# Strassen's scheme in the second MLP product of the four-block chunks (sliding-window attention and an MLP on one NeuronCore)

## The chip, the cores and the metric

The kernel runs on one core of a Trainium2 chip. The metric is device time in microseconds (us) of one execution, lower is better. Three runs of the kernel before took 319.13, 319.74 and 320.32 us; their median is 319.74.

The engines are named as in the profile: PE is TensorE (PEld its weight loads), DVE is VectorE, ACT is ScalarE, POOL is GpSimd, SP is SyncE, which here only issues DMAs. Each engine works through its own queue in order. PE writes its products to PSUM, in banks of 512 fp32 values per partition; the other engines take them from there.

## The reference

Attention over 8 batches, 8 heads, 576 positions and a head size of 64, in a window of 128 positions back with a linear bias for each head; its output, 4608 rows of 512, goes through a norm and a two-layer MLP of width 2048 and is added to the result:

```python
scores = np.where(mask, q @ k.T / sqrt(64) + bias, -1e9)     # mask: 0 <= rel < 128
x = softmax(scores) @ v                                      # 8 x 576 x 512
xn = (x - mean(x)) / sqrt(var(x) + 1e-6) * g_ln
out = x + np.maximum(xn @ w_ch1, 0.0) @ w_ch2                # w_ch1 512 x 2048, w_ch2 2048 x 512
```

## The kernel before

The 4608 rows are 36 blocks of 128. For each block `attention(i)` loads q, k and v, transposes q and k, makes the scores (L750, for the early blocks with a bias product at L766), their exponentials (ACT, L798), the masking product (DVE, L805), the weighted values (L822, two halves of four heads), and on DVE the division by the sums (L839, L843), the statistics (L864, L870) and the centred, scaled rows `xs` (L876, L883). `xs` is transposed into `xt`, for the first blocks on PE and later by a DMA from SP's queue (L912). The DMAs for q, k and v of the later blocks are cast in flight and issued from POOL's queue (L499); q and k of later blocks are transposed by DMA from SP's queue (L729).

The MLP (`mlp(c)`, L932) runs over ten chunks of 3, 3, 2 and then seven times 4 blocks. The first product, 16 groups of four matmuls (L944), makes 128 of the 2048 hidden columns each, for all rows of the chunk at once (512 columns of moving data in a four-block chunk). ACT or DVE applies the ReLU on the way from PSUM to `ht` in fp16 (L956, L954). The second product takes one block after the other: 16 matmuls of 512 columns (L972), with a 128x128 piece of `ht` as weights and a row piece of `w_ch2` (`w2sb`) as moving data, summed in one bank of PSUM. DVE scales the sum by the row's 1/std (the norm's division is left until here), adds `xb`, the attention output (L980, written `o` with the block's number), and SP's queue stores the result (L988). The last block's product is cut into 384 and 128 columns.

The order of all this is not written out. `Plan` is a list scheduler that runs when the program is built: every piece is a task with an engine or a choice of engines (`add(name, {"ACT": cost, "DVE": cost}, ...)`), the tasks that it waits for, and a due time `v`; for each engine the ready task with the earliest due time comes next. So an added task can change the order around it. The attention of a block has a due time some 1.6 chunks before that of its MLP, so in the middle of the kernel the attention of later blocks lies between the products of a chunk. `PRI`, `HOLD` and `PICK` are tables of hand-set corrections to due times, earliest starts and choices of engine, by the tasks' names.

PSUM has eight banks. `scs` are two tiles of two banks each for scores; `fb` are four banks for everything else: a task takes a bank with `acq` and the task named in `rel` frees it. A `Ring` is a set of buffers that are used in turn: the next use of a buffer waits for the readers of the last. `ht` has two buffers, `ot` (the output rows) four, `xs` three, `qkt` (transposed q and k) six and more for single blocks.

Of the kernel before, what the change touches and what calls it, by code (L numbers as in the profile page):

```python
# [241 lines left out]
def kernel(  # L242
# [17 lines left out]
    NKB = d_model // P  # L260
    NFB = ffn // P
    HP = H // 2
    NBLK = B * S // P
    PERIOD = 2 * S // P
    CB = 4
    CH = CB * P
    CHUNKS = [3, 3, 2, 4, 4, 4, 4, 4, 4, 4]
    FIRST = [sum(CHUNKS[:c]) for c in range(len(CHUNKS))]
# [38 lines left out]
    def sb(name, shape, dt):  # L307
        return pool.tile(shape, dt, tag=name, name=name)
# [10 lines left out]
    iden32 = sb("iden32", [P, P], FP32)  # L319
    sid = sb("sid", [P, H, P], FP16)  # L320
    dist_t = sb("dist_t", [P, 3, 2 * P], FP16)
# [11 lines left out]
    k32 = ring("k32", 2, [P, H, D if single else 1], FP32)  # L333
    v32 = ring("v32", min(4, V_CAST), [P, H, D], FP32)
    qk16 = ring("qk16", 5, [P, 2, d_model], FP16)
    vx = ring("vx", 7 if V_CAST > 4 else 9, [P, H, VD], FP16, FAR)
    qkt = ring("qkt", 6, [P, 2, HP, P], FP16, FAR)
    qs = ring("qs", 2, [P, H, 2 * D], FP32)
    ks = ring("ks", 2, [P, H, 2 * D], FP32)
    qs16 = ring("qs16", 2, [P, H, D, 2], FP16)  # L340
    ks16 = ring("ks16", 2, [P, H, D, 2], FP16)
    probs = ring("probs", 3, [P, 4, 2, 2 * P], FP16)
# [3 lines left out]
    ht = ring("ht", 2, [P, NFB, CH], FP16)  # L346
    ot = ring("ot", 4, [P, d_model], FP32)
    st = ring("st", 4, [P, nc.vector.BN_STATS_DIM], FP32)
# [5 lines left out]
    mean = ring("mean", 4, [P, 1], FP32)  # L354
    g_row, one_t = ot[3][0:1, :], ot[2][0:1, 0:P]

# [8 lines left out]
    def av(i, stage=0.0):  # L365
        return (i / CB - LEAD) * SPAN + stage
# [187 lines left out]
    def weights(i, casts):  # L554

        for n, at in enumerate(W_AFTER):
# [9 lines left out]
            t_w[n] = plan.transfer(f"w{n}", "POOL", 0.8, (3.2 if n else 4.2) if n < 4 else 2.7, 0.0, emit, [casts[at % 3]] + last, av(i, -60.0))  # L566

    span_done, pv_done, qkt_part, first_turn = {}, {}, {}, []
    qkt_done, vx_done, aggr_done, xs_done, xt_done = {}, {}, {}, {}, {}

    def attention(i):
# [49 lines left out]
        if i < V_CAST:  # L621
            cv = [add(f"cv{i}", pick("cv", "POOL", POOL=0.64, ACT=0.62), e_cv, lv_, av(i, 0.2))]
            v32.reads(i, cv[0]); vx.writes(i, cv[0])
        else:
            cv = lv_
# [9 lines left out]
        if i in span_of:  # L635
            n = span_of[i]
            if SPANS[n] == i:
                evs, casts = [[], []], {}
                for (a, x), (landed, h0, h1) in span_load[n].items():
                    r_, w_ = ((qs, qs16), (ks, ks16))[a]  # L640

                    def e_c(e, b, r_=r_, w_=w_, n=n, h0=h0, h1=h1):
                        dst = w_[n][:, h0:h1, :, :].rearrange("p h d t -> p t h d")
                        src = r_[n][:, h0:h1, :].rearrange("p h (t d) -> p t h d", t=2)
                        if e == "ACT":
                            nc.scalar.activation(out=dst, in_=src, func=AF.Copy)
                        else:
                            (nc.vector if e == "DVE" else nc.gpsimd).tensor_copy(out=dst, in_=src)  # L648
                    f = (h1 - h0) / H
                    cs = add(  # L650
                        f"cT{i}.{a}{x}", pick(f"cs{a}{x}", "POOL", POOL=0.12 + 1.26 * f, ACT=0.22 + 1.18 * f, DVE=0.1 + 0.7 * f),
                        e_c, [landed], av(i, 0.1 * a + 0.2 * x),
                    )
                    r_.reads(n, cs); w_.writes(n, cs)
                    for y in range(2) if f == 1 else (x,):
                        casts[a, y] = cs
                for x in range(2):
# [10 lines left out]
                    first_turn.append(tt)  # L668
                    qs16.reads(n, tt); ks16.reads(n, tt)
                    for blk in range(2):  # L670
                        def e_ev(e, b, x=x, blk=blk, key=key):
# [105 lines left out]
        for halves in ((0,), (1,)) if i < SPLIT else ((0, 1),):  # L777
# [4 lines left out]
            if bias:  # L782
                z_ = [add(f"Z{tag}{i}", ("PE", (0.87 if r else 0.46) * part), e_z(halves), t_sid + d_dist[kind > 0], av(i, 1.5 + 0.6 * halves[0]), acq=acq)]
            st_ = add(f"S{tag}{i}", ("PE", 0.19 + (0.45 if r else 0.23) * part), e_s(halves), z_ + qkt_part[i][halves[0]] + ([] if r == 0 else qkt_part[before][halves[0]]), av(i, 2.0 + 0.6 * halves[0]), acq=acq)
            qkt.reads(i, st_)
# [132 lines left out]
        if j == CHUNKS[c] - 1:  # L918
# [11 lines left out]
            kept[c] = rs  # L930

    def mlp(c):  # L932
        nb = CHUNKS[c]
        n_ = nb * P
        done = [xt_done[FIRST[c] + n] for n in range(nb)]
        v0, per = FIRST[c] / CB * SPAN, nb / CB * SPAN / 32
        relu = []
        for f in range(NFB):
            key = f"A{c}.{f}"
            vm = v0 + f * per  # L940

# [16 lines left out]
            ht.writes(c, r_)  # L958
            relu.append(r_)
        for j in range(nb):  # L960
            i = FIRST[c] + j
            cuts = (0, 3 * P, d_model) if i == NBLK - 1 else (0, d_model)
            for c0, c1 in zip(cuts, cuts[1:]):
                key = f"B{i}" if c1 - c0 == d_model else f"B{i}.c{c0}"
                last = None
                for f0 in range(0, NFB, 4):
                    vm = v0 + 16 * per + (4 * j + f0 / 4 + c0 / 100) * SPAN / 32

                    def e_b(e, b, j=j, f0=f0, key=key, c0=c0, c1=c1):
                        pm = fb[plan.held[key][1]]  # L970
                        for f in range(f0, f0 + 4):
# [3 lines left out]
                            )  # L975
                    last = add(f"{key}.{f0}", ("PE", 0.864 * (c1 - c0) / d_model), e_b, relu[f0 : f0 + 4] + [t_w[4 + f0 // 4][1], last], vm, acq=("fb", key))
                    ht.reads(c, last)
# [21 lines left out]
    for n, (at, tasks) in enumerate(cast_seq):  # L999
        before = [t_w[m][0] for m, w_at in enumerate(W_AFTER) if (w_at // 3 * 3 + 2 if w_at // 3 in span_of else w_at) < at][-1:] + (cast_seq[n - 1][1] if n and at < 3 * LOAD_CAST else [])  # L1000
        for t in tasks:
            t.deps += before
    t_g.deps.append(first_turn[0])
    for c in range(len(CHUNKS)):
        mlp(c)
# [46 lines left out]
```

## Time and profile before

| what | us |
|---|---|
| median of three runs (319.13 to 320.32) | 319.74 |
| span of the profiled execution | 317.5 |
| ScalarE busy in it | 161.0 |
| GpSimd busy in it | 100.6 |
| second product, L972, all forms: busy | 134.6 |
| first product, L944, all forms: busy | 134.5 |
| weighted values, L822, from `vx`: busy | 27.2 |
| scores, L750, largest two groups: busy | 18.0 and 14.7 |
| output step on VectorE, L980, all forms: busy | 27.2 |
| division, L843, and masking, L805 (all forms): busy | 30.3 each |

The profile is of one execution; the span goes from its first to its last instruction, and a run's time lies some 2 us above it. A line such as `L972 PE MATMUL fb<-w2sb,ht 128*128 128x512 f16 x560 | 131.6, 379 | 0.1` names the source line, the engine, the operation, what it writes from what it reads, the shape (128 partitions, 512 columns), the count, busy us and mean ns of one, and the engine's idle time before. Matmuls overlap in PE's pipeline, so the mean of one is longer than the time that one adds. In the chain, each piece has its start, its length, the engine and the line.

### The profile page before, as it was taken

How to read it: one execution, taken by the hardware profiler on the slowest of the kernel's cores; microseconds unless marked ns; L12 is line 12 of the kernel's file. 1: busy time of each engine (PE TensorE's matmuls, PEld its weight loads, DVE VectorE, ACT ScalarE, POOL GpSimd, SP SyncE). 2: the span in 40 equal slices, each digit the busy share in tenths (PEclk: the TensorE clock that was granted, in tenths of full speed). 3: DMA queues.
4: the chain of work that ended last, by engine and by line, in shares of the span. 5: the costliest groups of instructions: out<-in, count | busy, mean ns of one | idle time of the engine just before them, and what ended most of it. 6: DMA issues, size and time to landing. Idle time of an engine off the chain costs nothing.

```text
span 317.5 us, 6575 instructions
## 1 busy us (share of the span) xinstructions
PE 311.3 (98%) x2580; PEld 178.3 (56%) x2580; DVE 189.5 (60%) x523; ACT 161.0 (51%) x258; POOL 100.6 (32%) x133
## 2 busy tenths in 40 slices
PE   8999999999999999999999999999999999999995
PEld 7777656765955544555555555545555455445543
DVE  3496788889866646764676467648654676221012
ACT  3657816872836732674267426742574257305600
POOL 5663469765633355434263234000000000000000
PEclk9999999999999999999999999999999999999999
DMA  8999999999999999999999999834600240011011
GB/s 176 248 219 205 196 140 167 168 148 117 162 178 158 174 138 173 171 166 131 171 189 154 100 135 172 108 52 116 118 17 19 83 85 18 21 66 66 2 66 66
DMA packets 156049, 40.15 MB, mean 126 GB/s; under 512 B 142577, under 2 KB 151025, under 8 KB 156018
## 3 DMA queue, kind: packets, MB, share of 16 engines
q0 software_dynamic: 101680, 16.65, 75.7%
q1 hardware_dynamic: 54336, 23.08, 40.9%
q8 instruction: 20, 0.33, 0.5%
q14 instruction: 11, 0.09, 0.1%
q10 hardware_dynamic: 2, 0.00, 0.0%
HBM read 36.70 MB, written 9.44 MB: 145 GB/s over the span
## 4 chain that ended last, share of the span: by engine, by line
PE 91%; DMA 5%; DVE 1%; SPq 0%; POOL 0%; issue 0%
PE fb L944 40%; PE fb L972 39%; PE sc L750 6%; PE fb L822 5%; DMA vxp<-in_v_dram 3%; DMA qs<-in_q_dram 2%; PE fb L714 1%; PE fb L1011 0%; SPq L483 0%; PE fb L897 0%; PE sc L766 0%; PE fb L666 0%; POOL qs L648 0%; POOL w1sb L562 0%; DVE mmix L469 0%
## 5 line engine op out<-in xcount | busy, mean ns | idle before, releaser
L972 PE MATMUL fb<-w2sb,ht 128*128 128x512 f16 (+2 forms) x592 | 134.6, 373 | 0.1
L944 PE MATMUL fb<-xt,w1sb 128*128 128x512 f16 (+2 forms) x640 | 134.5, 359 | 0.0
L956 ACT ACTIVATE ht<-fb 128x512 f16<-128x512 f32 (+2 forms) x142 | 79.5, 560 | 52.4 <-PE fb L944 50.7
L798 ACT ACTIVATE probs<-sc 128x1024 f16<-128x1024 f32 (+1 forms) x72 | 67.8, 973 | 69.2 <-PE sc L750 69.0
L944 PEld LDWEIGHTS <-w1sb 128*128 128x128 f16 x640 | 68.9, 114 | 47.1
L972 PEld LDWEIGHTS <-ht 128*128 128x128 f16 x592 | 54.0, 98 | 57.4 <-issue 0.3
L980 DVE SCALAR_TENSOR_TENSOR ot<-fb,rstd,xb 128x512 f32<-128x512 f32 (+2 forms) x37 | 27.2, 736 | 42.1 <-PE fb L972 41.8
L499 POOL DMA_DIRECT2D vx<-in_v_dram x36 | 30.4, 849 | 38.0 <-PE fb L822 21.1
L499 POOL DMA_DIRECT2D qk<-in_q_dram x34 | 28.5, 839 | 42.7 <-DMA qkt<-qk 22.6
L805 DVE TENSOR_TENSOR probs<-probs,mreg 128x1024 f16<-128x1024 f16 (+1 forms) x46 | 30.3, 676 | 13.9 <-ACT probs L798 13.7
L839 DVE RECIPROCAL rec<-fb 128x4 f32<-128x4 f32 x72 | 12.7, 179 | 36.7 <-PE fb L822 36.4
L822 PEld LDWEIGHTS <-probs 128*128 128x128 f16 x544 | 24.9, 97 | 13.1 <-issue 0.6
L843 DVE SCALAR_TENSOR_TENSOR xb<-fb,rec 128x256 f16<-128x256 f32 x72 | 30.3, 422 | 1.9
L499 POOL DMA_DIRECT2D qk<-in_k_dram x34 | 28.7, 847 | 7.0 <-DMA qk<-in_k_dram 2.1
L883 DVE SCALAR_TENSOR_TENSOR xs<-xb,mean,g_t 128x512 f16<-128x512 f16 x36 | 26.9, 748 | 0.7
L822 PE MATMUL fb<-vx,probs 128*128 128x65 f16 x496 | 27.2, 193 | 0.1
L864 DVE BATCH_NORM_STATS2 st<-xb 128x6 f32<-128x512 f16 x36 | 24.6, 683 | 0.0
L750 PEld LDWEIGHTS <-qkt 64*128 64x128 f16 x496 | 14.9, 94 | 11.9 <-issue 10.1
L750 PE MATMUL sc<-qkt 64*128 64x128 f16 x264 | 18.0, 216 | 0.0
L750 PE MATMUL sc<-qkt,qkt 64*128 64x128 f16 x208 | 14.7, 219 | 0.0
L954 DVE TENSOR_SCALAR ht<-fb 128x384 f16<-128x384 f32 (+2 forms) x18 | 10.4, 579 | 6.3 <-PE fb L944 6.0
L1011 PE MATMUL fb<-warm_t 128*128 128x128 f16 x122 | 10.6, 251 | 1.1 <-DVE warm_t L400 1.1
(71 smaller groups left out, 128.6 us busy)
## 6 DMA issues: line engine op xcount, KB each, us to landing
out_dram<-ot SPq DMA_DIRECT2D x35, 256.0 KB, 4.0
vx<-in_v_dram POOLq DMA_DIRECT2D x28, 128.0 KB, 9.8
qk<-in_q_dram POOLq DMA_DIRECT2D x26, 128.0 KB, 9.2
qk<-in_k_dram POOLq DMA_DIRECT2D x26, 128.0 KB, 10.1
w1sb<-in_moe_w_ch_dram POOLq DMA_DIRECT2D x4, 512.0 KB, 11.1
w2sb<-in_moe_w_ch_dram POOLq DMA_DIRECT2D x4, 512.0 KB, 14.2
ks<-in_k_dram SPq DMA_DIRECT2D x4, 256.0 KB, 6.5
qs<-in_q_dram SPq DMA_DIRECT2D x4, 256.0 KB, 6.2
```

The costliest lines, as they stand in the source:

```text
L499: nc.gpsimd.dma_start(out=dst(p0, n), in_=src[b, :, s0 : s0 + n, :].rearrange("h p d -> p h d"))
L750: nc.tensor.matmul(scs[half][:, g, c0 : c0 + P], kt[rows, 1, hp, :], qkt[i][rows, 0, hp, :], start=not bias, stop=True, skip_group_check=True,
L798: nc.scalar.activation(out=o, in_=n_, func=AF.Exp, scale=inv_sqrt_d)
L805: en.tensor_tensor(out=pv, in0=pv, in1=mask[:, 2 * half : 2 * half + 2, :, lo:], op=ALU.mult)
L822: nc.tensor.matmul(pp[:, hh * (D + 1) : hh * (D + 1) + D + 1], probs[i][:, bank, slot, side * P : side * P + P], vx[i if side else before] ...
L843: nc.vector.scalar_tensor_tensor(out=xb[i][:, 256 * half : 256 * half + 256].rearrange("p (h d) -> p h d", d=D), in0=pp[:, :, 0:D], scalar ...
L864: nc.vector.bn_stats(out=st[i][:, :], in_=xb[i][:, :])
L883: nc.vector.scalar_tensor_tensor(out=xs[i][:, :], in0=xb[i][:, :], scalar=mean[i][:, 0:1], in1=g_t[:, :], op0=ALU.subtract, op1=ALU.mult,)
L944: nc.tensor.matmul(fb[b][:, 0:n_], w1f[f // CB][:, kb, f % CB, :], xt[c][:, kb, 0:n_], start=(kb == 0), stop=(kb == NKB - 1),)
L956: nc.scalar.activation(out=ht[c][:, f, 0:n_], in_=src, func=AF.Relu)
L972: nc.tensor.matmul(pm[:, 0 : c1 - c0], ht[c][:, f, j * P : j * P + P], w2sb[f // CB][:, f % CB, c0:c1], start=(f == 0), stop=(f == NFB - 1),)
L980: nc.vector.scalar_tensor_tensor(out=ot[i][:, c0:c1], in0=fb[plan.held[key][1]][:, 0 : c1 - c0], scalar=rstd[c][:, j : j + 1], in1=xb[i][: ...
```

## The change

For the seven four-block chunks the second product becomes one step of Strassen's scheme (in Winograd's form). The chunk's `ht` is seen as a matrix of four quarters: rows of its first two blocks and its last two (`lo_`, `hi_`), hidden columns 0 to 1023 and 1024 to 2047; `w_ch2` as four quarters too: the two halves of the hidden rows and of the 512 columns. Seven products of quarters (P1 to P7) take the place of eight. Each is 2 blocks x 8 hidden tiles = 16 matmuls of 256 columns.

- `weight_sums` makes four quarter sums of `w2sb` (`tw`, eight DVE instructions of 128x1024 fp16), once.
- `second` makes four quarter sums of `ht` in each chunk: `s3`, `s2`, `s1` (in place, over the lower left quarter) and `s4`, each in two halves of the hidden tiles, so eight DVE instructions of 128x1024 fp16. A half waits for the ReLUs of its eight hidden tiles, and the ReLUs of the second half end with the last one of the chunk.
- The products share four banks: P1 and then P2 in bank a, P6 and P7 in b, P5 and P3 in c, P4 in d. Between two products of one bank the first's value is taken out: `t1` copies P1 (ACT or DVE), `u2` = P6 + t1, `u3` = (P6 + P7) + t1, `v22` = P5 + u3, `v21` = P4 + u3, `v12` = (P5 + P3) + u2, all fp32 on DVE from PSUM, 512 columns at once (two blocks).
- Finishing steps (scale, add `xb`): `o11` for P1 + P2 from PSUM and `o12` from SBUF, 256 columns for each of two blocks, `o2`, 512 columns from SBUF, for each of the other two.
- The order of the products is 1, 6, 2, 7, 5, 4, 3. In the last chunk it is 1, 6, 7, 5, 4, 3, 2, each product is split by block, c and d are the score banks, and the results of the first two blocks are stored in two halves.
- The first product's hidden tiles are made in the order 0, 8, 1, 9, ... .
- To make room, the buffers `qs`, `ks`, `qs16`, `ks16`, `sid` and `v32` of the early blocks share their memory with the sums; `gate` holds the sums until all early users are done.

The planner gives every choice among the finishing steps to DVE, and all `t1` to ACT. `PRI`, `HOLD` and `PICK` stay as they are.

```diff
-    CHUNKS = [3, 3, 2, 4, 4, 4, 4, 4, 4, 4]
+    FOLDED = {c for c, n in enumerate(CHUNKS) if n == 4}
...
+    def weight_sums():
+        for m in range(2):
+            part = [t[:, CB * m : CB * m + CB, :] for t in tw]
+            landed = [t_w[4 + m][1], t_w[6 + m][1]]
+            steps = (
+                (0, quarter(0, 1, m), quarter(0, 0, m), ALU.subtract, None),
+                (1, quarter(1, 1, m), part[0], ALU.add, 0),
+                (2, quarter(0, 1, m), quarter(1, 1, m), ALU.add, None),
+                (3, quarter(1, 0, m), part[1], ALU.subtract, 1),
+            )
...
+    def second(c, relu, v0):
+        for g in range(2):
+            f_, f2 = slice(CB * g, CB * g + CB), slice(HFB + CB * g, HFB + CB * g + CB)
+            ready = [relu[f] for f in range(CB * g, CB * g + CB)] + [relu[HFB + f] for f in range(CB * g, CB * g + CB)]
+            steps = (
+                ("s3", s3[:, 0, f_, :], h[:, f_, hi_], h[:, f_, lo_], []),
+                ("s2", s3[:, 1, f_, :], h[:, f2, hi_], s3[:, 0, f_, :], ["s3"]),
+                ("s1", h[:, f_, hi_], h[:, f_, hi_], h[:, f2, hi_], ["s3"]),
+                ("s4", s3[:, 2, f_, :], h[:, f2, lo_], s3[:, 1, f_, :], ["s2"]),
+            )
...
+        PRODUCTS = {
+            1: ("a", hq(0, 0), w2q(0, 0), None, None),
+            2: ("a", hq(0, 1), w2q(1, 0), None, None),
+            6: ("b", sq(1), tq(1), "s2", 1),
+            7: ("b", sq(0), tq(2), "s3", 2),
+            5: ("c", hq(1, 0), tq(0), "s1", 0),
+            3: ("c", sq(2), w2q(1, 1), "s4", None),
+            4: ("d", hq(1, 1), tq(3), None, 3),
+        }
+        last_one = c == len(CHUNKS) - 1
+        wide_banks = "cd" if last_one else ""
+        groups = [[p] for p in range(np_)] if last_one else [list(range(np_))]
+        order_ = (1, 6, 7, 5, 4, 3, 2) if last_one else (1, 6, 2, 7, 5, 4, 3)
...
+                                nc.tensor.matmul(
+                                    pm[:, k_ * HALF_D : k_ * HALF_D + HALF_D], left(f, p), right(f),
+                                    start=begins and k_ == 0 and f == 0, stop=f == HFB - 1, skip_group_check=True,
+                                )
...
+                    nc.vector.tensor_tensor(out=dst, in0=a, in1=i1, op=ALU.add)
+                return add(name, ("DVE", 0.14 + 0.55 * share), emit, deps, vv, rel=keys[x] if rel and x not in wide_banks else None)
...
+                    t_["u"] = after["b"] = vec(f"u2{c}.{gn}", "b", tile_of["t"], tile_of["u"], [tail, t_["t"]] + gate, v - 4.0)
...
+                    t_["w"] = vec(f"u3{c}.{gn}", "b", tile_of["t"], tile_of["w"], [tail, t_["t"]] + gate, v - 4.0, rel=True)
...
+                            nc.vector.scalar_tensor_tensor(out=dst, in0=src, scalar=scale, in1=xb[i][:, c0:c1], op0=ALU.mult, op1=ALU.add)
...
     def mlp(c):
...
+        for at, f in enumerate([f for n in range(HFB) for f in (n, n + HFB)] if folded else range(NFB)):
...
+        if folded:
+            second(c, relu, v0 + 16 * per)
+            return
         for j in range(nb):
```

## The prediction

> **What bounds the kernel now.** I read the page's busy shares and slices first, then the chain that ended last, then the windows by stage, then the groups with the shapes kept apart, then pieces of the timeline.
>
> ```profile
> span 317.5 us, 6575 instructions
> PE 311.3 (98%) x2580; PEld 178.3 (56%) x2580; DVE 189.5 (60%) x523; ACT 161.0 (51%) x258; POOL 100.6 (32%) x133
> ...
> PEclk9999999999999999999999999999999999999999
> ```
>
> TensorE (PE) is busy 98% of the span at the full granted clock. A busy PE need not be at its peak, so the chain has to say whether the products themselves fill the time. Its last three pieces are two second products with a first product between them, 64 matmuls each (80 in the last, where one block is cut in two):
>
> ```profile
> 272.50 13.81 PE fb L972 x64
> 286.31 13.81 PE fb L944 x64
> 300.13 13.87 PE fb L972 x80
> ```
>
> 13.81 / 64 = 0.216 us for a matmul of 512 columns, with no gaps. So a matmul removed from the second product (L972) shortens the span by its own time, as long as nothing else becomes late. The windows show who might:
>
> ```profile
> core 0: us, PE busy (x) PEld busy (x) DVE busy (x) ACT busy (x) POOL busy (x), PEclk, DMA share, GB/s
> ...
> 49.20:80.00 30.80, 30.80 (x350) 20.05 (x349) 27.94 (x80) 19.33 (x29) 22.35 (x28) 1.00 2.27 151
> ...
> 160.70:193.00 32.30, 32.30 (x258) 16.90 (x256) 20.43 (x53) 16.71 (x26) 14.60 (x18) 1.00 1.56 145
> ...
> 272.50:286.30 13.80, 13.80 (x66) 6.26 (x64) 2.25 (x3) 0.68 (x2) 0.00 (x0) 1.00 0.12 43
> ```
>
> 160.7 to 193 is one whole period of a four-block chunk: VectorE (DVE) works 20.43 of 32.30 us. From 49 to 80 us it is 91% busy. These two rows carry the argument.
>
> **The change part by part.** The prices come from these rows (mean ns of one) and pieces:
>
> ```profile
> L972 PE MATMUL fb<-w2sb,ht 128*128 128x512 f16 x560 | 131.6, 379 | 0.1
> ...
> L805 DVE TENSOR_TENSOR probs<-probs,mreg 128x1024 f16<-128x1024 f16 x44 | 29.4, 687 | 13.0 <-ACT probs L798 12.9
> ...
> L980 DVE SCALAR_TENSOR_TENSOR ot<-fb,rstd,xb 128x512 f32<-128x512 f32 x35 | 26.3, 750 | 41.9 <-PE fb L972 41.5
> ...
> L954 DVE TENSOR_SCALAR ht<-fb 128x512 f16<-128x512 f32 x5 | 3.5, 692 | 0.8 <-PE fb L944 0.8
> ...
> L805 DVE TENSOR_TENSOR probs<-probs,mreg 128x512 f16<-128x512 f16 x2 | 0.9, 426 | 0.9 <-ACT probs L798 0.8
> ...
> L980 DVE SCALAR_TENSOR_TENSOR ot<-fb,rstd,xb 128x384 f32<-128x384 f32 x1 | 0.6, 618 | 0.0
> ...
> L980 DVE SCALAR_TENSOR_TENSOR ot<-fb,rstd,xb 128x128 f32<-128x128 f32 x1 | 0.4, 351 | 0.2 <-PE fb L972 0.2
> ```
>
> ```profile
> 83.82 2.79 PE L944 MATMUL fb<-xt,w1sb 128*128 128x256 f16 x24
> ...
> 129.17 1.28 DVE L805 TENSOR_TENSOR probs<-probs,mreg 128x1024 f16<-128x1024 f16 x2
> ...
> 314.02 0.35 DVE L980 SCALAR_TENSOR_TENSOR ot<-fb,rstd,xb 128x128 f32<-128x128 f32 x1 [0.22 <-PE fb L972]
> ```
>
> *Matmuls.* Per chunk 64 matmuls of 512 columns go and 7 x 2 x 8 = 112 of 256 columns come, each with its own 128x128 weights. The first product of the two-block chunk has just this shape: 24 took 2.79 us, of which some 0.2 is the pipe's tail (one 512-column matmul is shown with 0.379 but costs 0.216), so 0.108 each: the weight load hides at this width too. 13.81 - 112 x 0.108 = 13.81 - 12.10 = 1.71 us per chunk, seven chunks: **-12.0 us**. Bounds: without the tail's deduction a matmul is 0.116, 112 x 0.116 = 13.0, and the gain shrinks to 5.7; above 12.1 nothing excludes little.
>
> *VectorE work per chunk.* Added: eight sums of 1024 half-precision elements (s1 to s4, two halves each), 0.64 (two in 1.28) to 0.687, 5.1 to 5.5 us; five 512-wide adds from PSUM (u2, u3, v22, v21, v12), between L954's 0.692 and L980's 0.750, 3.5 to 3.75; four finishing steps of 256 (o11, o12), halfway between 0.351 and 0.618, 1.9; two of 512 from SBUF (o2), 1.5. Removed: four L980, 3.0, and one ReLU of 0.69 that VectorE took per period and the new order leaves to ScalarE. Net 8.3 to 9.0. So 28.7 to 29.4 us of work in a period of 32.3 - 1.7 = 30.6: 94 to 96%. I take 29.1. It still fits, but in-order queues at 95% do not stay hidden.
>
> *Waits that this makes.* I laid one chunk's new order on both queues by hand, zero being the first matmul of the second product, attention pieces between at 0.24 (weighted values, half a block) and 0.5 (scores). VectorE cannot start the second half of the sums before the last ReLU (0.2 for the hand-over, as before the 128-wide L980, and 0.60 for L956 after zero); at its prices it ends u2 at 5.5, both o11 at 9.95, u3 at 10.65, v22 at 11.7, v21 at 14.4, o12 at 18.65. TensorE wants u2 at 6.2 (late by nothing), the bank that o11 frees at 9.9, the bank that u3 frees at 10.3, the bank under v22 at 12.9. The four PSUM banks of fb are the point: the seven products hold three or four of them, and the matmuls for P4 queue behind the u3 that frees one. Stalls: 0.15 + 0.4, about **0.6 us** a chunk. Behind the waiting matmul stand attention scores, for which ScalarE waits with slack. VectorE then needs 11.6 us more before the next chunk's last ReLU, done at about 30.3 of 31.4: it catches up each period, so the stalls do not accumulate. Five chunks (the fourth to the eighth) have attention inside their second product: 5 x 0.6 = **+3.0**; bounds 0 and 5 x 1.7 = 8.5 (the stall eats the gain), taken near the walk. In the ninth no attention competes (2.25 us of VectorE work in 13.8): its gain is whole.
>
> *Weight sums, once.* Eight sums, 8 x 0.64 = 5.1 us, stand in VectorE's queue right where the first outputs (o0 to o2) are made, about 43 to 52 us, where the timeline has it idle 0.44 + 1.10 + 0.41 = 1.95. The order moves ReLUs and one copy to ScalarE, but about 3 us of lag stays. TensorE meets it as late banks: o0 to o2 hold three of four, and first-product groups then turn over one bank. I take **+1.5**, from two or three groups that wait 0.5 to 0.7 each; bounds 0 (hidden) and 5.1 (all on the path). From 80 to 112 us VectorE has 11 us free and the lag is gone.
>
> *Copies.* t1 (0.60, as L956's 512 columns) goes to ScalarE, busy 16.7 of 32.3 us, and is wanted only by u2 and P2: nothing; 0.6 a chunk if that cover were gone.
>
> *SP's queue.* The number of transfers is nearly the same (37 to 38 stores), but the four stores of a chunk now stand together behind o12, with the transposes of xs and qk behind them. Those are for two chunks and some seven blocks later, and held up by some 5 us; landing takes 6.4 and 9.0 (page, medians): nothing. Without that lead each 5 us would be TensorE's.
>
> *The end.* The last chunk's adds lie in the path: after the last matmul VectorE still has v12's rest, both o12 and the last o11, about 1.5 us against 0.37 now (last matmul at 314.0, 0.35 step shown above), and some 0.2 for waits on v22. **+1.3**; bounds 0.3 and 2.
>
> POOL's DMA issues (L499, median 0.88 us) lie beside eight L805 per four blocks already and show no stretch (0.68 to 0.97). The Trainium skill (SBUF — State Buffer, "Who interferes with whom") speaks against the change here: an instruction of VectorE with two SBUF inputs contends with GpSimd's SBUF reads, and the later one waits for the whole of the earlier. By that each chunk's eight sums could hold POOL up by 8 x 0.69 = 5.5 us, in a queue that is busy 14.6 of 32.3; by the row nothing; the sum is the same by both.
>
> **Sum.** -12.0 + 3.0 + 1.5 + 1.3 = -6.2 on the profiled execution: 317.5 - 6.2 = 311.3. The median of the runs, 319.74, lies 2.24 above the span; so **313.5 us**.
>
> **Rivals.**
> *No stall* (0.17): every wait hides. For it: VectorE's remaining 1.5 us a period, and ready work behind. Against: the o11 and u3 meetings above. 319.74 - 12.0 + 1.3 = 309.0.
> *The weight sums lie wholly on the path* (0.10): for it, the 91% window. Against: second-product work of three blocks that TensorE can do meanwhile. 313.5 + 3.6 = 317.1.
> *VectorE's lag decides, through the banks* (0.19): if the real hand-overs between engines keep VectorE 1 to 2 us later than my walk at u3, each of the five chunks stalls 2.6 rather than 0.6: 313.5 + 10 = 323.5, slower than before. It decides from (12.0 - 1.5 - 1.3) / 5 = 1.85 us a chunk. For it: 95%, one bank to spare. Against: the lag is worked off in each first product.
> *The sums run at one element per cycle* (0.04): by the slope between L980's 128 and 512 columns, 0.40 / 384 = 1.04 ns, a sum would be 0.22 + 1024 x 0.00104 = 1.28 and VectorE's period 34.2, 1.9 over the old one: five chunks and the weight sums give about 319.74 + 9.5 + 5 = 334. Against: the strided 512-element L805 at 426 and the 1024 at 687 differ by 0.51 ns an element. It decides from 1.03 a sum.
>
> **How the numbers follow.** The forecast (stalls of 0.2 to 1.1 a chunk, 311 to 316) has 0.50. A difference of 0.5%, 1.6 us, is what can be told from none: faster is below 318.1, slower above 321.3. Faster: 0.50 + 0.17 and half of the case of the weight sums, 0.72; same: its other half and the mild end of the bank case, 0.08; slower: the rest of that and the last case, 0.20. Range: 308.5 to 321, which leaves out little below and, above, most of the two slow cases.
>
> **What would show it.** TensorE's second products as 256-column groups at 0.108; VectorE near 95% in the middle periods, of some 31 us each; TensorE idle or the product's line waiting for VectorE's u3 and o11 by under 1 us a chunk; the last product at 12.1 to 12.5 and the end about 1.1 us later behind it. I am wrong if the sums take over 0.8 us, if 256-column matmuls take 0.12, or if TensorE's waits for VectorE come to more than 9 us.

## The result and the profile after

The changed kernel took 311.22 us (median of four runs, 310.41 to 311.91), the kernel before beside it 319.57: a ratio of 0.974 (95% interval 0.9718 to 0.9762), 8.35 us less. The profiled execution spans 309.5 us, 8.0 less than before. Forecast were 313.5, and 311.3 for the span.

The page of the changed kernel, its head:

```profile
span 309.5 us, 7349 instructions
PE 300.2 (97%) x2900; PEld 210.1 (68%) x2900; DVE 242.0 (78%) x636; ACT 166.6 (54%) x270; POOL 100.9 (33%) x133
```

VectorE has 52.5 us more to do (242.0 against 189.5), TensorE 11.1 less, and TensorE is still busy nearly all the time. Line numbers moved: the first product is now L1162, the seven products L1059, the plain second product of the early chunks L1193 with its output step L1201; VectorE's weight sums are L969, the sums of activations L992, the adds from PSUM (u and v) L1041, the finishing steps L1107, masks L824, the division by the softmax sums L858 and L862. The chain of the changed kernel, at the first group of products of the folded chunks:

```profile
114.13 2.62 PE fb L1059 x24
...
144.81 2.62 PE fb L1059 x24
...
175.49 2.62 PE fb L1059 x24
...
266.38 10.48 PE fb L1059 x96
...
292.50 2.62 PE fb L1059 x24
```

24 matmuls of 256 columns in 2.62 us and 96 in 10.48 are 0.1092 each. These starts (with 205.70 and 236.38 between those shown) are the best measure of the change, because they show where the time went. In the kernel before the same chunks started as follows, and then at 208.66, 240.92, 272.50 and 300.13:

```profile
112.37 2.59 PE fb L972 x12
...
144.62 2.59 PE fb L972 x12
...
176.87 2.59 PE fb L972 x12
```

| stretch | before | after | difference |
|---|---|---|---|
| up to the first folded chunk's second product | 112.37 | 114.13 | +1.76 |
| to the next chunk's, six times | 32.25, 32.25, 31.79, 32.26, 31.58, 27.63 | 30.68, 30.68, 30.21, 30.68, 30.00, 26.12 | -1.57, -1.57, -1.58, -1.58, -1.58, -1.51 |
| from the last one's start to the end of the span | 17.37 | 17.00 | -0.37 |
| sum | 317.5 | 309.5 | -8.0 |

13.81 - 112 x 0.1092 = 1.58 is what the matmuls alone give a chunk. So in the middle the gain arrives whole (0.07 is missing in the ninth chunk; no run shows why). The windows say the same, here of the whole period of the fifth chunk, first after the change and then before it:

```profile
core 0: us, PE busy (x) PEld busy (x) DVE busy (x) ACT busy (x) POOL busy (x), PEclk, DMA share, GB/s
144.81:175.49 30.68, 30.68 (x306) 21.71 (x305) 26.91 (x67) 17.73 (x28) 12.69 (x16) 1.00 1.64 152
```

```profile
144.62:176.87 32.25, 32.25 (x257) 16.90 (x256) 20.44 (x53) 16.66 (x26) 13.77 (x17) 1.00 1.80 158
```

TensorE is busy 30.68 of 30.68 us. VectorE works 26.91 us, 88%, where 94 to 96% were forecast; the same period before had 20.44 of 32.25, so 6.5 us came on top and not 8.3 to 9.0. The groups of the new instructions, with the shapes kept apart (busy, mean ns of one):

```profile
L992 DVE TENSOR_TENSOR early<-ht,early 128x1024 f16<-128x1024 f16 x28 | 19.1, 683 | 1.6 <-ACT ht L1174 0.3
...
L1041 DVE TENSOR_TENSOR ot<-fb,scrap 128x512 f32<-128x512 f32 x18 | 12.3, 689 | 3.5 <-PE fb L1059 3.4
...
L1107 DVE SCALAR_TENSOR_TENSOR ot<-fb,rstd,xb 128x256 f32<-128x256 f32 x14 | 6.1, 474 | 2.7 <-PE fb L1059 2.7
```

The durations are those that the forecast took (0.64 to 0.687, 0.692 to 0.750, 0.48). What differs is how the instructions follow each other. A piece of VectorE's timeline (start, length):

```profile
145.46 0.69 DVE L992 TENSOR_TENSOR early<-ht 128x1024 f16<-128x1024 f16 x1
146.25 0.69 DVE L992 TENSOR_TENSOR early<-ht,early 128x1024 f16<-128x1024 f16 x1
146.85 0.68 DVE L992 TENSOR_TENSOR ht<-ht 128x1024 f16<-128x1024 f16 x1
147.46 0.68 DVE L992 TENSOR_TENSOR early<-ht,early 128x1024 f16<-128x1024 f16 x1
```

Each is shown with 0.68 to 0.69 us, but the next one starts 0.60 to 0.61 us after it, unless it needs the result of the one directly ahead (0.79 between the first two: s2 reads s3). The durations overlap by 0.08 us, as those of the matmuls do. The Trainium skill has this (Perfetto Trace Analysis, "Optimizing Scalar/DVE Operations"): the fixed overhead of such an instruction shows in the profiled latency with about twice the time for which it holds the engine, since the part for the acknowledgement of its write overlaps the next instruction. The trace agrees that there is such an overlap, with 0.60 against 0.69.

Over the whole period this is the difference to the forecast. The lengths of VectorE's records add up to 30.42 us in it, and to 22.04 in the kernel before: 8.4 more, as forecast. But 3.5 us of the 30.42 are overlaps, against 1.6 before, and the busy time counts those once.

Behind the last matmul, at about 304.9 us, VectorE's timeline has the rest of the last chunk's steps:

```profile
304.24 0.76 DVE L1041 TENSOR_TENSOR ot<-sc,scrap 128x256 f32<-128x256 f32 x2 [0.60 <-PE sc L1059]
304.92 0.87 DVE L1107 SCALAR_TENSOR_TENSOR ot<-ot,rstd,xb 128x256 f32<-128x256 f32 x2
305.70 0.48 DVE L1107 SCALAR_TENSOR_TENSOR ot<-fb,rstd,xb 128x256 f32<-128x256 f32 x1
```

They end at 306.18. Behind its start the last product gained 1.58 and the span 0.37, so the end is 1.2 us longer than before.

### The profile page after: what moved, and what is told of

The parts are those of the page before. It is cut to its first block, busy times and chain, and to the rows that moved or that the text cites. A ratio compares the mean times of both kernels' runs of the same rounds, so it can differ in the third digit from the quotient of the medians.

```text
span 309.5 us, 7349 instructions
## 1 busy us (share of the span) xinstructions
PE 300.2 (97%) x2900; PEld 210.1 (68%) x2900; DVE 242.0 (78%) x636; ACT 166.6 (54%) x270; POOL 100.9 (33%) x133
## 4 chain that ended last, share of the span: by engine, by line
PE 84%; DMA 8%; DVE 5%; issue 1%; SPq 0%; POOL 0%; DVEq 0%
PE fb L1162 39%; PE fb L1059 26%; PE fb L1193 5%; PE sc L768 5%; PE fb L841 5%; DMA vxp<-in_v_dram 4%; DMA qkt<-qk 3%; DMA early<-in_q_dram 2%; PE sc L1059 1%; DVE early L969 1%; PE fb L732 1%; DVE ot L1041 1%; PE fb L1233 1%; DVE ot L1201 0%; DVE probs L824 0%
## 5 line engine op out<-in xcount | busy, mean ns | idle before, releaser
L1162 PE MATMUL fb<-xt,w1sb 128*128 128x512 f16 (+2 forms) x640 | 136.5, 359 | 0.5 <-DVE ot L1201 0.5
L1174 ACT ACTIVATE ht<-fb 128x512 f16<-128x512 f32 (+2 forms) x145 | 81.0, 568 | 59.5 <-PE fb L1162 57.8
L1162 PEld LDWEIGHTS <-w1sb 128*128 128x128 f16 x640 | 68.5, 114 | 44.3 <-issue 0.7
L1059 PEld LDWEIGHTS <-ht 128*128 128x128 f16 x448 | 42.4, 98 | 7.0 <-issue 0.4
L824 DVE TENSOR_TENSOR probs<-probs,mreg 128x1024 f16<-128x1024 f16 (+1 forms) x46 | 30.5, 668 | 7.7 <-ACT probs L817 7.7
L1059 PEld LDWEIGHTS <-early 128*128 128x128 f16 x336 | 32.4, 98 | 5.8
L1193 PE MATMUL fb<-w2sb,ht 128*128 128x512 f16 x128 | 31.2, 379 | 0.2 <-DVE xb L862 0.2
L862 DVE SCALAR_TENSOR_TENSOR xb<-fb,rec 128x256 f16<-128x256 f32 x72 | 30.1, 419 | 1.0
L1059 PE MATMUL fb<-w2sb,ht 128*128 128x256 f16 x224 | 29.2, 273 | 0.0
L992 DVE TENSOR_TENSOR early<-ht,early 128x1024 f16<-128x1024 f16 x28 | 19.1, 683 | 1.6 <-ACT ht L1174 0.3
L1193 PEld LDWEIGHTS <-ht 128*128 128x128 f16 x128 | 11.5, 98 | 11.6 <-issue 0.4
L858 DVE RECIPROCAL rec<-fb 128x4 f32<-128x4 f32 x72 | 12.6, 176 | 7.1 <-PE fb L841 6.6
```

The lines of the kernel that those rows point to most:

```text
L824: en.tensor_tensor(out=pv, in0=pv, in1=mask[:, 2 * half : 2 * half + 2, :, lo:], op=ALU.mult)
L862: nc.vector.scalar_tensor_tensor(out=xb[i][:, 256 * half : 256 * half + 256].rearrange("p (h d) -> p h d", d=D), in0=pp[:, :, 0:D], scalar ...
L1059: nc.tensor.matmul(pm[:, k_ * HALF_D : k_ * HALF_D + HALF_D], left(f, p), right(f), start=begins and k_ == 0 and f == 0, stop=f == HFB - 1 ...
L1162: nc.tensor.matmul(fb[b][:, 0:n_], w1f[f // CB][:, kb, f % CB, :], xt[c][:, kb, 0:n_], start=(kb == 0), stop=(kb == NKB - 1),)
L1174: nc.scalar.activation(out=ht[c][:, f, 0:n_], in_=src, func=AF.Relu)
L1193: nc.tensor.matmul(pm[:, 0 : c1 - c0], ht[c][:, f, j * P : j * P + P], w2sb[f // CB][:, f % CB, c0:c1], start=(f == 0), stop=(f == NFB - 1),)
```

## The experiments

All times are medians; ratios are to the kernel before, timed on the same chip beside them. "Period" means from one folded chunk's second product to the next one's, as in the table above. Where a kernel has a line more or two, its line numbers are one or two higher.

### What a 256-column matmul costs

The kernel before, its 512-column matmuls of the four-block second products cut in two, or in four:

```diff
-    nc.tensor.matmul(pm[:, 0 : c1 - c0], ht[..], w2sb[.., c0:c1], start=(f == 0), ..)
+    for h0 in (0, 256):
+        nc.tensor.matmul(pm[:, h0 : h0 + 256], ht[..], w2sb[.., c0 + h0 : c0 + h0 + 256], start=(f == 0 and h0 == 0), ..)
```

> The kernel before, with every 512-column matmul of the four-block second products cut into two of 256 columns, each with its own weights; nothing else moves. Theory (a 256-column matmul costs 0.1092 us, as the chain of the changed kernel shows with 24 in 2.62 and 96 in 10.48): 13.81/128 = 0.1079 is half of a 512-column one, so 7 x 128 x 0.0013 = 1.2 us more, 320.8. Rival (0.108, the price of the forecast, and the rest of the shortfall lies elsewhere): no change, 319.6.

> The same cut into four of 128 columns, each with its own weights. Theory 1 (each matmul costs its columns and a fixed 2.6 ns: 0.2158 and 0.1092 lie on 0.0026 + columns x 0.000416): 0.0559 each, four are 0.0077 dearer than one of 512, 7 x 64 x 0.0077 = 3.5 us more, about 323. Theory 2 (the weight load, 210.1/2900 = 72 ns on average in the changed kernel, is the floor under a matmul this narrow): four cost 0.29, 0.072 more than 0.216, 448 x 0.072 = 32 us more, about 352. It tells whether halving once more would still pay.

Cut in two: 321.02 us (before 319.42), ratio 1.0054 (1.0033 to 1.0075), 1.6 us more. Cut in four: 323.48, ratio 1.0133 (1.0109 to 1.0157), 4.1 us more. One second product in the chain of each:

```profile
273.98 13.97 PE fb L974 x128
```

```profile
275.70 14.29 PE fb L975 x256
```

13.97 / 128 = 0.1091 and 14.29 / 256 = 0.0558, where one of 512 columns costs 0.2158. The three lie on a line: 0.00042 us a column and about 0.0025 for each matmul. Per chunk the cut costs 0.16 and 0.48 us, seven times 1.1 and 3.4 (the intervals begin at 1.1 and 3.5; of the profiles' spans another 0.7 us lies ahead of the first cut matmul, where the kernels are alike). So the price 0.108 of the forecast was 0.0012 too low, and the 72 ns of the second expectation (the busy time of all weight loads over their count) is no floor: at 128 columns a matmul with its own weights still comes every 56 ns. (The weight loads are then busy all the time, 14.24 of 14.30 us; narrower was not tried.) By these prices (an estimate) a second step of the scheme would lose only this small fixed part on TensorE.

### Do the sums reach TensorE at all?

The changed kernel with the activation sums' instructions left out and their products reading plain quarters; all queues else unchanged.

```diff
-                def emit(e, b, o=o, a=a, b_=b_):
-                    (nc.vector if e == "DVE" else nc.gpsimd).tensor_tensor(out=o, in0=a, in1=b_, op=ALU.subtract)
+                emit = None
```

> The changed kernel without the eight activation sums of each chunk; the products that used them read activations as they are, so that what is computed differs, and every other instruction keeps its order. VectorE has 8 x 0.60 = 4.8 us less to do in a period of 30.7. Theory (in the changed kernel nothing of the sums reaches TensorE: seven chunks gain 1.58 each, as the matmuls alone give): same time as the changed kernel, periods within 0.1 of 30.7 and 30.2, 310.9 to 311.4. Rival (the forecast's 0.6 us a chunk of stalls is there): five chunks shorter by 0.6, about 308.2.

310.66 us, ratio 0.9724 (0.9688 to 0.9759). The periods are 30.67, 30.68, 30.22, 30.68, 29.99 and 26.12, against 30.68, 30.68, 30.21, 30.68, 30.00 and 26.12 with the sums. The period shown above, in this kernel:

```profile
144.39:175.07 30.68, 30.68 (x306) 21.73 (x305) 22.40 (x59) 17.73 (x28) 12.41 (x16) 1.00 1.34 134
```

4.5 us less VectorE work (22.40 against 26.91), and TensorE's time is the same to 0.01. The forecast's 0.6 us of stalls a chunk does not exist, and 308.2 falls with it. GpSimd's DMA issues take 846 to 851 ns here and 850 to 857 with the sums, so the sums held GpSimd up by nothing that shows. The rule of the Trainium skill that the prediction weighed against this (SBUF — State Buffer, "Who interferes with whom") is about GpSimd instructions that read SBUF; the same section says that `tensor_tensor` did not stall DMAs where it was tried, and these rows agree with that.

### How much more VectorE work would it have taken?

The changed kernel with sums done twice: three of the four in each half, or only the last.

```diff
+                    for _ in range(2 if name in ("s3", "s2", "s4") else 1):
                         (nc.vector if e == "DVE" else nc.gpsimd).tensor_tensor(out=o, in0=a, in1=b_, op=ALU.subtract)
```

> The changed kernel with three of the four activation sums (s3, s2, s4) of each half computed twice: six VectorE instructions a chunk more, 6 x 0.60 = 3.6 us in a period of 30.7 with 26.9 busy, so 30.5 of 30.7. Nothing else moves. Theory 1 (VectorE's lag turns into late PSUM banks under the products, the forecast's slow rival): the three extra ones of the second half delay the fifth and seventh product's adds by 1.8 us, of which 0.2 to 0.7 is slack, so about 1.4 us a chunk in the five chunks with attention beside them, +6 to +8 us, 317 to 319. Theory 2 (what counts is only that VectorE's work fits in the period): under 1 us more.

> The changed kernel with the last activation sum (s4) of each half computed twice: two VectorE instructions, 1.2 us, more a chunk, a third of what the six extra ones added. Theory 1 (VectorE is part of the loop, so that of the 3.8 us it has free in a period only about one can be used, since the rest is waiting for ScalarE's probabilities: six extra ones cost 2.8 us a period for 3.6 to 3.9 us of work): 0.2 to 0.5 a period, 1 to 2.5 us more, 312.2 to 313.7. Theory 2 (nothing is lost until the free 3.8 us are used up): no change, 311.2. Theory 3 (every added microsecond is lost, in proportion to the 16 us for six): 5 us more, 316.

Six more a chunk: 327.27 us, ratio 1.0243 (1.0225 to 1.0261), 16 us above the changed kernel and slower than the kernel before. Two more: 313.75, ratio 0.9802 (0.9776 to 0.9829), with periods 0.30 to 0.44 longer. Both are nearer to the first theory, but for six it was far too mild: the five periods with attention grew by 2.8, 2.8, 2.0, 4.3 and 3.2, twice what was expected. TensorE's waits in the kernel with six more, from 112 to 290 us (total, times, longest):

```profile
PE fb L841 <- DVE xb L862: 5.8, 5, 1.2
PE fb L1163 <- DVE xb L862: 4.7, 5, 1.1
PE fb L1060 <- DVE early L993: 2.5, 5, 1.6
```

The first two are not about the products' banks u3 and o11: TensorE waits for the step that normalises the weighted values (L862), which frees their bank. The late sums come third. So there is no room for 3.6 us at this place, though VectorE had 3.8 us free.

### Is it the load, or the place?

Three kernels tell this apart. The seventh product's add done twice (0.60 us more, ahead of the bank that the forecast took for the tight one):

```diff
+                    for _ in range(2 if name[:2] == "u3" else 1):
                         nc.vector.tensor_tensor(out=dst, in0=a, in1=i1, op=ALU.add)
```

> The changed kernel with the add of the seventh product (u3, 0.60 us, whose end frees the PSUM bank that the forecast saw as the tight one) done twice in each chunk. Theory 1 (the tight place is that bank: the walk through the changed kernel's fourth chunk leaves 0.2 to 0.7 us there): 0.25 to 0.4 a period and more, 1.5 us and more in all, 312.7. Theory 2 (only the load counts: 1.2 us of extra sums cost 0.30 a period, 3.6 cost 2.8, so some 0.9 to 1.0 is absorbed): 0.60 is absorbed, periods of 30.7 as before, 311.2.

Two sums (1.2 us, result unused) behind the last output step of a chunk:

```diff
                             nc.vector.scalar_tensor_tensor(out=dst, in0=src, scalar=scale, in1=xb[i][:, c0:c1], op0=ALU.mult, op1=ALU.add)
+                            for _ in range(2 if name[:3] == "o12" and j == 1 and not last_one else 0):
+                                nc.vector.tensor_tensor(out=spare, in0=w2sb[0][:, :, 0:HALF_D], in1=w2sb[1][:, :, 0:HALF_D], op=ALU.add)
```

> The changed kernel with two sums more (1.2 us of VectorE, result unused) in each chunk, as in the run with s4 twice, but behind the chunk's last output step, some 17 us after the second product's start, where VectorE next stands idle 1.56 us waiting for ScalarE. Theory 1 (the load counts, wherever it stands): the same 0.30 a period as with s4 twice, 1.5 us in all. Theory 2 (the place counts): the idle 1.56 us behind it takes up the 1.2, 0 to 0.1 a period, 311.2 to 311.7, unless the normalising steps that stand between, and that free the banks of the weighted values, become late; then TensorE shows waits for VectorE at the line of the weighted values or of the first product.

And the same two sums some instructions later, directly ahead of the mask for which VectorE waits:

```diff
+    for c in range(4, 9):
+        s_at = next(n for n, x in enumerate(order) if x[0].name == f"s3{c}.0")
+        mask = max(n for n in range(s_at) if order[n][1] == "DVE")
...
+        order.insert(mask, (extra, "DVE", None))
```

> The changed kernel with the same two extra sums (1.2 us of VectorE, result unused) in five chunks, now directly ahead of the mask at which VectorE of the changed kernel stands idle 1.56 us for ScalarE's probabilities, that is behind the normalising steps and ahead of the next chunk's activation sums. Theory 1 (the place counts: behind the output steps the same 1.2 us cost 0.71 a period, because the normalising steps that free the banks of the weighted values came late, with s4 twice 0.30): here nothing waits behind them, 0 to 0.1 a period, 311.2 to 311.7. Theory 2 (the load counts, some 0.5 to 0.9 us of spare and no more): 0.3 to 0.7 a period, 312.7 to 314.7.

| kernel | VectorE more per chunk | period more, us | time, us | ratio (interval) |
|---|---|---|---|---|
| s4 twice, ahead of u3 | 1.2 | 0.31, 0.31, 0.30, 0.44, 0.31, then 0 | 313.75 | 0.9802 (0.9776 to 0.9829) |
| u3 twice | 0.60 | 0.39, 0.40, 0.40, 0.14, 0.39, then 0.73 | 314.98 | 0.9845 (0.9813 to 0.9877) |
| behind the output steps | 1.2 | 0.72, 0.71, 0.72, 0.73, 0.71, then 0 | 314.40 | 0.983 (0.9804 to 0.9856) |
| ahead of the mask | 1.2 | 0, 0, 0, 0.13, 0, 0 | 311.11 | 0.9745 (0.9712 to 0.9778) |

The windows of one period with the two sums behind the output steps, and of the same period with them ahead of the mask:

```profile
144.72:176.11 31.39, 30.84 (x307) 21.72 (x305) 28.12 (x69) 17.73 (x28) 12.67 (x16) 1.00 1.38 131
```

```profile
143.93:174.61 30.68, 30.68 (x306) 21.72 (x305) 28.18 (x69) 17.73 (x28) 12.70 (x16) 1.00 1.48 144
```

VectorE works 28.12 and 28.18 us, the same, yet TensorE stands 0.55 us in the first and not at all in the second. So it is the place and not the load; ahead of the mask VectorE is 92% busy and costs nothing. What is behind the two sums shows in VectorE's timeline of the first:

```profile
162.13 1.41 DVE L1110 TENSOR_TENSOR scrap<-w2sb,w2sb 128x1024 f16<-128x1024 f16 x2
...
164.14 0.41 DVE L862 SCALAR_TENSOR_TENSOR xb<-fb,rec 128x256 f16<-128x256 f32 x1
```

and in TensorE's:

```profile
164.60 1.89 PE L1165 MATMUL fb<-xt,w1sb 128*128 128x512 f16 x8 [0.56 <-DVE xb L862]
```

The first product needs a bank that the weighted values still hold, and the extra sums stand ahead of the step that frees it. The u3 row shows that the forecast's tight place is real. In the fifth chunk of that kernel:

```profile
153.81 1.41 DVE L1042 TENSOR_TENSOR scrap<-fb,tu 128x512 f32<-128x512 f32 x2
155.27 0.93 PE L1060 MATMUL fb<-early,ht 128*128 128x256 f16 x7 [0.24 <-DVE scrap L1042]
```

The two adds end at 155.22, and the matmuls that need the bank start 0.05 later. The pair takes 1.41 us where the single add takes 0.68, so the bank comes free 0.73 later; in the changed kernel it was free 0.38 before it was wanted, and TensorE is late by 0.4, in four of the five chunks with attention. The medians differ by 3.8 us, over twice the 1.5 expected. In the profile 2.4 of that are in the periods, with 0.73 in the ninth chunk, where no attention fills the wait, and 0.8 behind the last product's start. The changed kernel passes the place with little to spare, and passes it on time.

### Where the early 1.76 us are

Twice the eight weight sums were taken out of VectorE's queue at 43 to 51 us and put elsewhere, once spread out from 84 us on, once into the two places where VectorE stands idle.

```diff
     order = plan.run()
+    moved = [x for x in order if x[0].name[:2] == "tw"]
+    order = [x for x in order if x[0].name[:2] != "tw"]
...
+    order[mask:mask] = moved[6:]
+    order[at["o7.0"]:at["o7.0"]] = moved[:6]
```

> The changed kernel with its eight weight sums taken out of VectorE's queue at 43 to 51 us and put back one by one from about 84 us on; every other instruction of every engine stays in its order. Theory (the sums are what made the third chunk's second product start 1.76 us late): 1.3 to 1.8 us less, about 309.7, and the starts of all second products from the fourth chunk on earlier by as much. Rival (the late start comes from the other new orders, the ReLUs' order and the load of the transposed keys on SP's queue): less than 0.4 us, 310.9 to 311.3.

> The changed kernel with the eight weight sums moved once more: six of them to the place at 96 to 99.8 us and two to the place at 103.7 to 106.1 us where VectorE of the changed kernel stands idle (3.62 and 2.42 us); all else keeps its order. Theory (the sums' place is worth what the changed kernel's TensorE waits between 38 and 114 us: 0.46 for VectorE's output step, 0.50 for the transposed keys, 0.25 for the copy of the keys, 0.17 for the normalised block): 0.9 to 1.4 us less than the changed kernel, about 310.1. Rival (those waits come from the new orders of the other queues, and the later place in the run before lost only by chance of the read of the inputs): within 0.4 us of the changed kernel.

Spread out: 313.13 us, ratio 0.9799 (0.9778 to 0.982), worse than the changed kernel by 1.9. It was put among the ReLUs of the third chunk that VectorE does, and TensorE then waits 1.4 us for those. In the idle places: 312.0 us (310.04 to 313.33), ratio 0.9743 (0.9712 to 0.9774), no gain that shows; the least gain that the theory expected, 0.9, would be a ratio of 0.971, at the edge of the interval. TensorE's waits in the timeline between 40 and 116 us, changed kernel first:

```profile
43.60 1.89 PE L1193 MATMUL fb<-w2sb,ht 128*128 128x512 f16 x8 [0.17 <-DVE xb L862]
...
53.12 0.81 PE L1162 MATMUL fb<-xt,w1sb 128*128 128x384 f16 x4 [0.46 <-DVE ot L1201]
...
86.34 0.23 PE L768 MATMUL sc<-qkt,qkt 64*128 64x128 f16 x2 [0.50 <-DMA qkt<-qk]
```

```profile
43.93 1.89 PE L1193 MATMUL fb<-w2sb,ht 128*128 128x512 f16 x8 [0.49 <-DVE xb L862]
...
83.16 0.23 PE L768 MATMUL sc<-qkt,qktp 64*128 64x128 f16 x2 [0.94 <-DMA qkt<-qk]
87.04 0.23 PE L768 MATMUL sc<-qkt,qkt 64*128 64x128 f16 x2 [0.47 <-DMA qkt<-qk]
```

Only the wait at the output step, 0.46 us, goes with the sums. In its place TensorE waits 0.94 for transposed q and k at the scores of 83 us. It reaches them only 0.2 us earlier than in the changed kernel (82.22 against 82.42), so the transfer landed later, and so did the next one, which both chains have:

```profile
77.05 9.25 DMA qkt<-qk
```

```profile
76.23 10.77 DMA qkt<-qk
```

It was issued 0.8 us earlier and landed 0.7 later; why it took longer no run shows. The rest of the 1.76 did not go with the sums.

Some of it is not the change's either. The changed kernel and eight of the kernels made from it have the same instructions up to some 106 us, and all start the same group of 16 matmuls in the fourth chunk's first product, each in its one profiled execution, at 100.18, 100.25, 100.30, 100.53, 100.64, 100.69, 100.74, 101.05 and 101.81; the changed kernel's is the 101.05. The kernel before and the two with cut matmuls, which are alike up to there, start it at 99.28, 99.97 and 100.08. By the means, 100.69 and 99.78, the early part costs some 0.9 us and not 1.76, though three and nine executions with this spread fix it loosely. What makes the part that does not go with the sums stays open; the new orders of the other queues are one candidate.

### The last chunk

Once left as it was before (`FOLDED` without the last chunk), once with a shorter end:

```diff
-        order_ = (1, 6, 7, 5, 4, 3, 2) if last_one else (1, 6, 2, 7, 5, 4, 3)
+        order_ = (1, 6, 7, 5, 4, 2, 3) if last_one else (1, 6, 2, 7, 5, 4, 3)
...
+                    def e_o12(e, b, j=pairs[0], src=tile_of["u"]):
+                        nc.vector.scalar_tensor_tensor(out=ot[first + j][:, HALF_D:], in0=psum_of("c"), scalar=rstd[c][:, j : j + 1], in1=src, op0=ALU.mult, op1=ALU.add)
```

> The changed kernel with the last of the seven chunks left as it was (64 matmuls of 512 columns, the end as before). The forecast's two terms for it: the end costs 1.3, by the two traces (last matmul to end of span 3.5 before, 4.6 after) 1.1 to 1.2; the last chunk's products gain 13.81 - 112 x 0.1092 = 1.58. So the last chunk as changed is worth 0.3 to 0.5 only, and this kernel is slower than the changed one by that, about 311.6. Rival (the longer end is stores that another queue hides): 1.5 us slower, 312.8.

> The changed kernel with the last chunk's end rearranged: the third product last and in one piece for each block, and the first block's rest of the sum scaled and added to the input before it ends, so that one VectorE step of 256 columns, not four, stands behind the last matmul. Theory (the end is those steps: last matmul to last step 1.3 us in the changed kernel, 0.7 here): 0.5 to 0.7 us less, 310.6. Rival (the row of six stores on SP's queue sets the end): no change, 311.2.

Left as before: 311.08 us, ratio 0.9735 (0.9712 to 0.9757); from the last second product's start to the end its profile has 17.4 us, 0.4 more than the changed kernel, as the first theory expected; the medians, 311.08 and 311.22, do not show it. The rival's 1.5 is excluded. With the shorter end: 310.75, ratio 0.9717 (0.9698 to 0.9736); the same stretch is 16.5, 0.5 less, as expected. The medians differ from the changed kernel's in that direction, by 0.47, but the intervals overlap. VectorE's only step behind the last matmul there:

```profile
305.10 0.48 DVE L1103 SCALAR_TENSOR_TENSOR ot<-sc,rstd,scrap 128x256 f32<-128x256 f32 x1 [0.69 <-PE sc L1064]
```

## Why the prediction was right, and where it was off

The direction and the range held, and so did the main term. The mechanism of the second largest term did not. That 311.2 still lies in the forecast's own band, 311 to 316, is in part luck: that band was for stalls of 0.2 to 1.1 us a chunk, and there were none. Without its 3.0 us of stalls the forecast is 310.5, and the 0.9 that it took too much for the matmuls happens to bring that back to the measured time. Its parts against what was measured:

| term | forecast | measured |
|---|---|---|
| matmuls, seven chunks | -12.0 | -11.1 (7 x 1.58, at 0.1092 each) |
| stalls in five chunks | +3.0 | 0 (periods with and without the sums agree to 0.01) |
| weight sums, early | +1.5 | +1.76 in the one profile, 0.9 by the means; one wait of 0.46 is the sums' own |
| the end | +1.3 | +1.2 |
| sum | -6.2 | -8.1 by these, -8.0 by the spans |

*Matmuls.* Right but for the tail that was taken off "24 took 2.79 us": 0.2 should have been 0.17 (one is shown with 273 ns and costs 109). The Trainium skill (TensorE: Matmul & The Clock Gate, "Wait — 56ns, not 53.3ns?") gives columns by the array's rate and some 2.5 ns on top, 109.2 and 55.8 ns as an estimate from it; the runs gave 109.1 and 55.8.

*Stalls.* This is the step that failed: "at its prices it ends u2 at 5.5, both o11 at 9.95, u3 at 10.65". The prices were the durations of single instructions, laid end to end and added to a busy time of 20.43 us in which overlaps count once. In the trace of the fifth chunk the first matmul is at 144.64. Both o11, then u3, and the matmuls that take u3's bank:

```profile
153.17 0.86 DVE L1107 SCALAR_TENSOR_TENSOR ot<-fb,rstd,xb 128x256 f32<-128x256 f32 x2
153.94 0.68 DVE L1041 TENSOR_TENSOR scrap<-fb,tu 128x512 f32<-128x512 f32 x1
```

```profile
155.00 1.03 PE L1059 MATMUL fb<-early,ht 128*128 128x256 f16 x8
```

Both o11 end at 154.03 and u3 at 154.62, 9.39 and 9.98 us after the first matmul, so 0.56 and 0.67 earlier than in the walk: the stalls that it found, 0.15 and 0.4, were no larger than that. TensorE wants u3's bank at 10.36 (10.3 in the walk) and does not wait. The walk's single steps are not on record, but the overlaps are large enough for the difference: the 19 records from the second half's first sum (145.46) to the second o11 add up to 9.42 us and take 8.57. That VectorE would be at 94 to 96% was wrong for the same reason. The chart of who waits for whom was right: a u3 that ended 0.73 us later cost 0.4.

*"In-order queues at 95% do not stay hidden."* Not so as it stands: with the two sums ahead of the mask VectorE is at 92% and hidden, with u3 twice at 89% (127.54 of 144 us) it is not. The share says little; the wait next in the queue says what a place costs.

*Weight sums.* The size came out near, the cause only in part as told: one bank, held by an output step, for 0.46 us, and not two or three. Moving the sums to idle time gained nothing that shows; in the one profile of that kernel transposed q and k, landing later, took the place of that wait.

*The end, t1, SP's queue, GpSimd.* As forecast. TensorE waits for no transfer in the middle periods.

*The rivals.* "No stall" is what happened in the middle; its 309.0 left out the early term and took 0.9 too much for the matmuls. "VectorE's lag decides" was a fair danger: six sums more per chunk gave 327.27 us. It came in mostly through the banks of the weighted values (10.5 us of TensorE's waits against 2.5 for late sums) and not, as told, through u3. "One element per cycle" falls: a sum of 1024 elements takes 0.68 us. "Weight sums wholly on the path" falls with the 0.46.

## What to carry to other kernels

Add up an in-order engine's work by the distance between starts of instructions that follow each other directly, not by their durations: here 0.08 us an instruction made 88% look like 95% and stood behind 3 us of stalls that weren't there. Where work is added to an engine that others wait for, look at what stands behind it in the queue: the same 1.2 us cost 0.7 a period ahead of a step that frees a bank, and nothing ahead of a wait for another engine. Seven products for eight pays on TensorE nearly in full, as long as the matmuls stay wide enough that 2.5 ns each is small and the sums find such places.

## What the hardware showed that was not expected

- A weight load of 98 ns on average for each 128-column matmul (as the profile shows it) did not hold up matmuls that came every 56 ns; cut in four, the second product cost 0.48 us a chunk and not 4.6.
- The loss grows faster than the work added: 1.2 us more of sums cost 0.30 to 0.44 us a period with attention, 3.6 us cost 2.0 to 4.3.
- Nine executions of the same instructions reached the same point, about 100 us on, as much as 1.6 us apart, which is more than the 0.46 of the one wait that went with the weight sums.
